# Features of one batch by seven products, a thirtieth seven-product block, tap 0 in two column parts, and engine orders as a table

## The chip, the cores and the metric

The kernel runs on one core of a Trainium2 chip. A core has five engines that run side by side and meet only at semaphores: TensorE (PE; its weight loads are PEld in the profile), VectorE (DVE), ScalarE (ACT), GpSimd (POOL) and SyncE (SP), which here only issues DMAs. The metric is the device time of one execution in microseconds. Before the change it is 252.21 us, the median of 3 runs from 251.29 to 252.40 us.

## The reference

```python
B, T, D, K, U = 2, 4000, 512, 5, 8
h = sum(xp[:, i:i+T, :] @ w1[i] for i in range(5))        # 5 taps over 4000 rows
h = gelu(h)[:, ::2, :]                                    # 2000 rows stay
f = sum(hp[:, i:i+T1, :] @ w2[i] for i in range(5))
f = gelu(f)[:, ::2, :]                                    # 1000 rows stay
fe = f @ w_f                                              # (2, 1000, 512)
ge = g @ w_g                                              # (2, 8, 512)
j = tanh(fe[:, :, None, :] + ge[:, None, :, :])           # (2, 1000, 8, 512)
out = j @ w_o                                             # 16,000 rows of 512
```

All tensors are bf16. Two convolutions with stride 2 make the features `f`; a joint net adds eight vectors `ge` to each feature row, takes tanh and multiplies by `w_o`. The 16,000 joint rows are 125 tiles of 128.

## The kernel before

Activations stand transposed, channels on the 128 partitions and time along the columns, so that every product is a chain of matmuls over four channel blocks `k`, once for each output block `m`. The helper `mm` (L442) records such a chain as one op.

- **First rows of batch 0, directly.** Rows of `x` come in two pieces, `xr0` (128 partitions, 512 KB) and `xr1` (90 partitions, 360 KB). PE turns them with 32 small transposes (L520) into PSUM banks 4 to 7; two DVE copies (`xr0`) and two ACT copies (`xr1`) bring them to `xs`. Then the five taps run in the order 0, 4, 2, 1, 3, each as 16 matmuls of 432 columns (216 even and 216 odd outputs), summed in banks 0 to 3 (`direct`, L702).
- **The other rows.** `Triple` and `Unit` compute three neighbouring outputs of a stride-2, 5-tap convolution from nine chains instead of fifteen, with sums of inputs (`row`) and sums of weights (`w_x`, `w_t`) that DVE and ACT make first. Four triples do the first convolution, two the second; each has four units, one for each `m`. A unit writes PSUM, DVE adds (L530, L429), ACT applies gelu (L434).
- **Features.** `fe` multiplies `fT` by `w_f`: 4 output blocks times 2 time halves, each 4 matmuls of 501 columns, and one copy to `feT` by DVE (L755) or ACT. For batch 0 this stage stands between the convolutions and the joint stage; for batch 1 its eight chains, like the last three units of batch 1 ("conv pieces"), are put between joint blocks.
- **Joint.** ACT makes `tanh(feT + geT)` (L434, `jT` and `jX`), 64 stretches of 1000 columns. `Plain` multiplies one tile of 128 rows by `w_o`: 4 matmuls of 512 columns, one eviction. `Seven` does four tiles by a 2 by 2 block scheme with 7 products instead of 8: 28 matmuls of 256 columns. It needs four sums of tanh blocks (`ss`, L931, DVE or POOL), four sums of `w_o` blocks (`tw`, made once), three products that are copied to `sn` first (L862, L863), three DVE additions `og <- acc, sn` (L429) and one cast. There are 29 `Seven` blocks and 9 plain tiles, three of these at the end.

**Order of the work.** Every op is recorded in program order with its engine (or, in `flex`, a choice of engines), reads, writes and a cost. `edges` (L124) finds what has to wait for what. `schedule` (L175) is a list scheduler: it always takes the engine that can go on first and the most urgent op that is ready there; PE takes the earliest in program order. A string of nudges, one character an op, shifts the urgency. `emit` writes each engine's list with semaphore waits. An engine works through its list strictly in order.

Ops recorded with `pl.port = True` (the sums `ss` here) are planned so that DVE's and POOL's don't overlap (L226 to L231).

Of the kernel before, what the change touches and what calls it, by code (L numbers as in the profile page):

```python
# [50 lines left out]
class Psum:  # L51
# [6 lines left out]
    def pair(self, lo, step, n):  # L58
        ap = self.h[:, lo:lo + 2 * step].rearrange("p (s c) -> p s c", s=2)[:, :, 0:n]
        cells = np.unique(np.concatenate([np.arange(lo, lo + n), np.arange(lo + step, lo + step + n)]) // 512)  # L60
        return View(ap, cells, True)


class Op:
# [4 lines left out]
NUDGES = (  # L69
    "WWWWWWWWWWWWWWWWWWWWWWWWWWWWWWWWWWWWWWWWWWWWWWWWWWWWWWWWWWWWWWWWWWWWWWWWWWWWWWWZGRxV4s1q-S-zIwUDlPB1btjPJVWAWWfYOS-0KT0d"  # L70
    "dIkA-0yl2ZWWWWWWWWWWWyWWQEqWWMWWm8ddCa1B0-yn00WoWW2KtWW7WWPWWg8HCWeWW1mZWWDWW0WWakaF--VX-W0WWOrTWWXWWUWW5WwWWJ-4WW_WW-WW"
    "-5T00vmWGWW70RWW6WW-WWb-mtW4WWGlgWW0WW0WW6-a2YwvXTWiWWKSvWWsWWaWW0W-WW-n-WWcWW_WWjsHUAloWWWWWW5Jd-Pq-WBWWD-2WW4WWeWWw-S0"
    "0fmDvt3RUh-W-WWY--WW-WWAWWEX4iYejb0992kFIky15WNWW2tUWW6WWkWWfuUox0NRL-GW-WW_S8WWSWW4WW0-z4Oe-ByzWdWWh-eWWrWWXWWnLu0W0WWi"
    "8-WWHWWKWWBJ0VxX26uWSWWf1RWW-WWPWWTW-WWtS4WW1WWjWW9WWWW-Zk-d0WYWWq-pWWOWWWWWcO-AWNWW0pSWWQWWzWWPqIYZ---bW4WWi06WW-WW-WWl"
    "WWWWyWW46MD-WW7_0WlW0MW-W-eWZWwnW0Wb0WW_WWXWhWfWWrW-i0-S2VEu4WWsWWbWW0WW9qj9BWWqWW-WWWMe0z0WWoWWKWWWWW4WWsy092WWSWWWWWWL"
    "WWWWWZWW-WW-WWnWWSW0O-SrWWaWWZWWWHWWW8rzw6WWxWW-WWDWWkWWOwFlY6-WWPWWIWWWhWWWWWuoeb4WWYWWYWWiWWqWW7H3IDWWGWWIWWWsWW-n2WWy"
    "WWRWW0WW_WW9W4tRWWCWWLWWWEWWWWW00-X-WWpWWUWWxWWQWWjcm7aWW0WWqWWW-WWWGqTWWoWW-WWlWW-WFQ7DiWWEWWVWWW-WWWW00-g_sjWWUWW0WW-W"
    "W-WyN---WW-WW3WWWTWWc0zz-WWHWWwWWGWWsWp9TM-WWzWWLWWW0WWWyfWWDWW2WWAWWQWE7E0kWW-WWjWWW0WduWW0WWAWW4WWUWpxUpFWWlWW3WWWdWWW"
    "WWwWWOWWJWWLWlzPsiWWzWWoWWWyWg0EOWWqWWAWWqWW9E9XdWWNWW0WWWIWWWNG0-yKWWsWW8WWEWWbI0LPWW-WW6WWW0W1yWW8WWTWWhWWsI_qTWWqWWQW"
    "WWPWWWwBWW-WWrWW-WWpYyqiWWDWWZWWWUW49WW7WWdWWFWWp5_FFWWQWWWWWW6WWWdXE0WWLWWAWWrWW07LstWWWWWtWWWsWxEBY8cWW3WW1WWwWWOVPnsW"  # L80
    "W0WWJWWWOWWWGEWW0WWYWW-WWHCX_fWWmWWCWWW0WC4WWVWWFWWJWW0W-WW-j0WWrWWaWWWWW5WZ-WWfWWFWW1WWOWqW--rmWW5WWdWWWJWWWG-lSWWTWWPW"
    "WbWW0Rrw1WW-WWqWWWDWeXsFWW0WWpWWfWW82Id5WWkWWPWWW8WWW6EWWiWWYWWMWW7W1tSWWdWWkWWWeWx2WW3WW-WWMWWSUx45WWyWWYWWWFWWWWW3WWyW"
    "W-WWfWxWD-qzWW0WWJWWWcWWWTWWtWWrWWyWNWWWWzWWJWWW1WWUWW3WWXWWWhWW0WLWWiW")


class Plan:
# [88 lines left out]
    def schedule(self, pred):  # L175


        ops, HOP = self.ops, self.HOP
        n = len(ops)
        succ = [[] for _ in ops]  # L180
        for i, p in enumerate(pred):
            for j in p:
                succ[j].append(i)
        span = [o.cost + (4.0 if o.dma else 0.0) for o in ops]
        late, nextpe = [0.0] * n, 0.0
        for i in range(n - 1, -1, -1):
            t = min([late[s] - (HOP if pred[s][i] else ops[i].cost - span[i]) for s in succ[i]], default=0.0)
            if ops[i].eng == "pe":
                t = min(t, nextpe)
            late[i] = t - span[i]  # L190
            if ops[i].eng == "pe":
                nextpe = late[i]
        nudge = [0.1 * (ALPHABET.index(c) - 32) for c in NUDGES] if len(NUDGES) == n else [0.0] * n
        left = [len(p) for p in pred]
        ready = [0.0] * n
        free = {e: 0.75 for e in ("pe", "act", "dve", "pool", "sp")}
        cand = {e: [] for e in free}

        def engines(i):
            return ops[i].alt or (ops[i].eng,)  # L200

        for i in range(n):
            if not left[i]:
                for e in engines(i):
                    cand[e].append(i)
        order = {e: [] for e in free}
        wire, lock, start = 0.0, 0.0, [0.0] * n
        for _ in range(n):
            best = None
            for e, c in cand.items():  # L210
                if c:
                    t = max(free[e], min(ready[i] for i in c))
                    if best is None or t < best[0]:
                        best = (t, e)
            t, e = best
            now = [i for i in cand[e] if ready[i] <= t + 0.02]
            i = min(now, key=(lambda i: i) if e == "pe" else (lambda i: (0.15 * i + nudge[i], i)) if e in ("sp", "pool") else (lambda i: (late[i] + nudge[i], i)))
            for f in engines(i):
                cand[f].remove(i)
            order[e].append(i)  # L220
            o = ops[i]
            if o.alt:
                o.eng, (o.fn, o.cost), o.alt = e, o.alt[e], None
            start[i] = t
            free[e] = t + o.cost
            if o.port:  # L226
                if lock > t - 0.2 and e == "dve":
                    free[e] = max(t, lock) + o.cost + 0.2
                elif lock > t:
                    free[e] = lock + o.cost  # L230
                lock = free[e]  # L231
            end = free[e]
            if o.dma:
                wire = max(wire, t + 1.8) + o.wire
                end = max(wire, t + 2.0)
            for s in succ[i]:
                ready[s] = max(ready[s], end + HOP if pred[s][i] else free[e])
                left[s] -= 1
                if not left[s]:
                    for f in engines(s):  # L240
                        cand[f].append(s)
        self.start = start
        self.end = max(free.values())
        return order

    def emit(self, block, tail):
        nc, ops = self.nc, self.ops
        pred = self.edges()
        order = self.schedule(pred)
# [71 lines left out]
def bass_standalone__seq2seq_rnn_t_joint__speech_kernel(  # L321
# [25 lines left out]
    NA, N3 = 216, 262  # L347
# [9 lines left out]
    with ExitStack() as es:  # L357
# [33 lines left out]
        xq = [Buf(nc, f"xq{i}", [6, NK, 288], BF16, v.end - v.bytes) for i, v in enumerate((xs[1], w2_sb))]  # L391
# [22 lines left out]
        tw = at("tw", [4, 2, NT // 2], FP16, wg_sb.end - wg_sb.bytes)  # L414
        assert tw.end <= wg_sb.end
# [61 lines left out]
        came = [load_xr(rt) for rt in range(2)]  # L477
        act(warm[0:1], warm[1:2], ACT.Gelu_apprx_tanh)

        def load_w1(i):  # L480
            src = w1[i].rearrange("(k c) d -> c k d", c=P)
            if len(came) == 2:
                h = D // 2
                for sl in (slice(0, h), slice(h, D)):
                    o = pl.dma("sp", lambda e, sl=sl: e.dma_start(w1_sb[i, :, sl].ap, src[:, :, sl]), (), (w1_sb[i, :, sl],), nbytes=262144)
            else:
                o = load_w("sp", w1_sb[i], src)
                o.after.append(came[-3].idx)
# [657 lines left out]
```

## Time and profile before

| | |
|---|---|
| median of 3 runs | 252.21 us (251.29 to 252.40) |
| profiled execution | 252.07 us |
| its span on the core | 250.3 us |
| PE / DVE / ACT / POOL busy | 245.5 / 207.8 / 209.9 / 106.7 us |
| first tap matmul starts | 7.29 us |
| batch 0's features on PE | 119.0 to 125.8 us |
| POOL sums `ss` / DVE sums `ss` | 86 / 30 instructions |

The span is the time from the first to the last instruction; 1.8 us of the execution lie around it. Busy time counts an instruction from its start to its modelled end; instructions that overlap on an engine are counted once. So 32 chained matmuls that are started every 0.21 us show as one busy stretch, and the rate is read from the starts.

### The profile page before, as it was taken

How to read it: one execution, taken by the hardware profiler on the slowest of the kernel's cores; microseconds unless marked ns; L12 is line 12 of the kernel's file. 1: busy time of each engine (PE TensorE's matmuls, PEld its weight loads, DVE VectorE, ACT ScalarE, POOL GpSimd, SP SyncE). 2: the span in 40 equal slices, each digit the busy share in tenths (PEclk: the TensorE clock that was granted, in tenths of full speed). 3: DMA queues.
4: the chain of work that ended last, by engine and by line, in shares of the span. 5: the costliest groups of instructions: out<-in, count | busy, mean ns of one | idle time of the engine just before them, and what ended most of it. 6: DMA issues, size and time to landing. Idle time of an engine off the chain costs nothing.

```text
span 250.3 us, 5204 instructions
## 1 busy us (share of the span) xinstructions
PE 245.5 (98%) x1920; PEld 184.5 (74%) x1920; DVE 207.8 (83%) x346; ACT 209.9 (84%) x354; POOL 106.7 (43%) x109
## 2 busy tenths in 40 slices
PE   8999999999999999999999999999999999999995
PEld 4556888887666666667467878877778888888873
DVE  1599999968999997981528978899899999999763
ACT  2297799978969868963699998999999999999673
POOL 1000000000000000002429898598998999998910
PEclk9999999999999999999999999999999999999999
DMA  7999999988500052000002223422344444564547
GB/s 212 307 187 173 192 164 212 147 173 262 163 0 3 0 169 85 1 1 3 0 0 84 86 84 105 151 88 84 112 145 131 160 154 141 171 211 156 185 162 240
DMA packets 57392, 31.92 MB, mean 128 GB/s; under 512 B 33837, under 2 KB 57149, under 8 KB 57367
## 3 DMA queue, kind: packets, MB, share of 16 engines
q1 hardware_dynamic: 57367, 31.59, 48.2%
q8 instruction: 15, 0.25, 0.4%
q14 instruction: 10, 0.08, 0.1%
HBM read 7.71 MB, written 16.38 MB: 96 GB/s over the span
## 4 chain that ended last, share of the span: by engine, by line
PE 89%; DVE 4%; DMA 4%; ACT 1%; issue 1%; DVEq 0%
PE acc L442 89%; DMA w_sb<-in_w_dram 2%; DMA xr<-in_x_dram 1%; DVE ssum L429 1%; DVE ssum L530 1%; DVE w_t L429 1%; DVE row L429 1%; ACT hT L434 1%; ACT w_x L434 0%; ACT ost L434 0%; DVE w_x L429 0%; ACT sd L434 0%; DVEq L282 0%
## 5 line engine op out<-in xcount | busy, mean ns | idle before, releaser
L429 DVE TENSOR_TENSOR og<-acc,sn 128x512 bf16<-128x512 f32 x87 | 56.7, 680 | 5.4 <-PE acc L442 4.7
L434 ACT ACTIVATE jT<-feT,geT 128x1000 bf16<-128x1000 f32 (+6 forms) x56 | 51.3, 961 | 0.5 <-DVE feT L755 0.4
L442 PE MATMUL acc<-tw,ss 128*128 128x256 f16 x348 | 48.3, 273 | 0.0
L442 PEld LDWEIGHTS acc<-tw,ss 128*128 128x128 f16 x348 | 33.7, 98 | 7.0 <-issue 0.4
L931 POOL TENSOR_TENSOR ss<-jT 128x512 f16<-128x512 bf16 x26 | 31.4, 1218 | 11.8 <-ACT jT L434 9.2
L442 PE MATMUL acc<-row,w_sb 128*128 128x334 bf16 (+1 forms) x192 | 33.1, 295 | 0.0
L862 ACT ACTIVATE sn<-acc 128x512 f32<-128x512 f32 x51 | 30.6, 619 | 2.6 <-PE acc L442 2.3
L442 PE MATMUL acc<-wo_sb,jT 128*128 128x256 bf16 (+1 forms) x196 | 31.6, 288 | 0.0
L426 POOL MEMSET hT<- 128x8 bf16 (+2 forms) x6 | 0.7, 149 | 71.6 <-ACT hT L434 66.7
L442 PE MATMUL acc<-row,w_x 128*128 128x262 bf16 (+1 forms) x192 | 28.5, 290 | 0.2 <-ACT sd L434 0.2
L434 ACT ACTIVATE jX<-feT,geT 128x1000 bf16<-128x1000 f32 (+4 forms) x28 | 25.0, 919 | 0.0
L442 PEld LDWEIGHTS acc<-row,w_sb 128*128 128x128 bf16 x192 | 18.5, 98 | 6.7 <-DVE acc L530 0.3
L442 PEld LDWEIGHTS acc<-row,w_x 128*128 128x128 bf16 x192 | 18.6, 98 | 6.1 <-ACT sd L434 0.5
L442 PEld LDWEIGHTS acc<-wo_sb,jT 128*128 128x128 bf16 x196 | 19.1, 98 | 5.3
L434 ACT ACTIVATE sd<-acc 128x334 f32<-128x334 f32 (+1 forms) x48 | 20.3, 429 | 2.6 <-PE acc L442 2.1
L530 DVE SCALAR_TENSOR_TENSOR acc<-acc,sd 128x334 f32<-128x334 f32 (+1 forms) x24 | 11.6, 482 | 11.4 <-PE acc L442 11.4
L434 ACT ACTIVATE hT<-acc 128x262 bf16<-128x262 f32 (+2 forms) x36 | 15.4, 433 | 6.7 <-PE acc L442 6.6
L863 DVE COPY sn<-acc 128x512 f32<-128x512 f32 x26 | 17.6, 682 | 3.9 <-PE acc L442 3.9
L931 POOL TENSOR_TENSOR ss<-jX 128x512 f16<-128x512 bf16 x17 | 20.3, 1209 | 1.2 <-ACT jX L434 0.7
L931 POOL TENSOR_TENSOR ss<-jT,ss 128x512 f16<-128x512 bf16 x15 | 17.8, 1191 | 1.0 <-DVE ss L931 0.7
L442 PE MATMUL acc<-wo_sb,ss 128*128 128x256 bf16 x116 | 17.7, 273 | 0.0
L931 POOL TENSOR_TENSOR ss<-ss,jT 128x512 f16<-128x512 f16 x15 | 17.5, 1173 | 0.6 <-DVE ss L931 0.4
(105 smaller groups left out, 499.7 us busy)
## 6 DMA issues: line engine op xcount, KB each, us to landing
out_dram<-og SPq DMA_DIRECT2D x44, 256.0 KB, 2.2
w_sb<-in_w_dram SPq DMA_DIRECT2D x9, 512.0 KB, 5.1
out_dram<-og SPq DMA_DIRECT2D x14, 128.0 KB, 2.2
out_dram<-ost SPq DMA_DIRECT2D x7, 128.0 KB, 2.0
xr<-in_x_dram SPq DMA_DIRECT2D x1, 512.0 KB, 3.4
w_sb<-in_w_dram SPq DMA_DIRECT2D x2, 256.0 KB, 5.3
wf_sb<-in_w_f_dram SPq DMA_DIRECT2D x1, 512.0 KB, 3.7
wg_sb<-in_w_g_dram SPq DMA_DIRECT2D x1, 512.0 KB, 4.7
```

The lines of the kernel that those rows point to most:

```text
L426: pl.op("pool", lambda e: e.memset(v.ap, 0.0), (), (v,))
L429: pl.op(eng, lambda e: e.tensor_tensor(out=o.ap, in0=a.ap, in1=b.ap, op=op), (a, b), (o,), 0.02 + 2.14e-3 * o.ap.free_size() if eng == "po ...
L434: pl.op("act", lambda e: e.activation(o.ap, i.ap, func, scale=scale, bias=0.0 if bias is None else bias.ap), rd, (o,), o.ap.free_size() * ...
L442: ins = e.matmul(o.ap, lhsT=l.ap, rhs=r.ap, start=start and n == 0, stop=stop and n == len(pairs) - 1, skip_group_check=not check)
L530: pl.op(eng, lambda e: e.scalar_tensor_tensor(out=o.ap, in0=a.ap, scalar=f, in1=b.ap, op0=ALU.mult, op1=add), (a, b), (o,), vec_cost(o, (a ...
L862: pl.flex({"act": (lambda e: e.activation(o.ap, v.ap, ACT.Copy), 0.05 + n * 0.833e-3), "dve": (lambda e: e.tensor_copy(out=o.ap, in_=v.ap) ...
L863: "dve": (lambda e: e.tensor_copy(out=o.ap, in_=v.ap), 0.065 + n * 1.04e-3)}, (v,), (o,))
L931: fn = lambda e, o=S[i], x=x, y=y, op=op: e.tensor_tensor(out=o.ap, in0=x.ap, in1=y.ap, op=op)
```

## The change

1. **Tap 0 and the first loads.** The loads are issued as `xr0`, the first two channel blocks of tap 0's weights, `xr1`, the other two blocks, and then tap 4 without a wait; before, they were `xr0`, `xr1`, two column halves of tap 0, and tap 4 after `xr0` had landed. Tap 0 is done in columns 0 to 127 and 128 to 215 of each output half, and each in two halves of the channel blocks: 16 matmuls of 256 and 16 of 176 columns. The transposes of `xr1` stand inside it. The copies of even rows (`turn(0, 0)`, `turn(1, 0)`) are DVE's, those of odd rows ACT's.
2. **Features of batch 0** by a new class `Feature`, the 2 by 2 scheme with seven products: for each of two `m`, seven products of 2 matmuls with 504 columns. It needs four sums of feature blocks (DVE, 1008 elements), four sums of `w_f` blocks (`wfsums`, 512 elements, DVE or POOL), six PSUM results kept in `sn`, six DVE additions and two plain copies.
3. **Thirty `Seven` blocks** and 5 plain tiles instead of 29 and 9.
4. **Orders as a table.** `schedule` and the nudges go; `ORDER` lists each engine's ops by their numbers, two characters each.
5. `ge` is recorded two slots earlier, and the sums of `w_o` may be DVE's too.

Read with the ops' numbers in program order, the table begins as follows. PE: 8 warm-up matmuls, transposes of even and odd rows of `xr0`, tap 0 columns 0 to 127 (blocks 0, 1), transposes of `xr1`, tap 0 columns 0 to 127 (blocks 2, 3), tap 0 columns 128 to 215, taps 4, 2, 1, the `t2` chains of units 0 and 2, tap 3 with the `t2` chain of unit 1 in it, then the units, strongly mixed. ACT: the warm-up, `w_x[1]` of block 0, `w_t[1]` of blocks 0 and 1, the copy of `xr0`'s odd rows, `w_x[1]` of block 1, the copy of `xr1`'s odd rows. DVE: the two copies of even rows, then 15 weight sums, then the first row sum of triple 0. In the joint stage DVE has 50 of the sums `ss` and POOL 70; of the 90 copies to `sn` ACT has 56 and DVE 34; of the 30 casts to `og` ACT has 20 and DVE 10. Of the eight weight sums of `w_f` and `w_o`, POOL has two.

In the feature stage PE's order is: unit 5.0's `t1` and `s1`, then p1, p2, p5, p6 for m = 0, p1 for m = 1, p3 for 0, p2, p5, p6 for 1, p7 for 0, p3, p7 for 1, unit 5.1's `t2`, p4 for 0, unit 5.0's `t0`, p4 for 1, unit 5.0's `ti`, the first half of block S0's p1, `si`, the second half, `s0`, and then the first plain tile. DVE's is: feature sum 1, unit 5.0's first addition, feature sums 2 and 3, unit 5.0's second, the results k0 first half, k0 second half, k1 first half, one copy to `sn`, k2, k1, k3 second halves, k2, k3 first halves. ACT's is: five copies to `sn` with one gelu among them, and tanh of (v0, k0), (v1, k0), (v0, k1), (v0, k2), (v0, k3).

```diff
-NUDGES = (
...
+ORDER = {
+    "pe": (
+        "0X0Y0Z0a0b0c0d0e0f0h0l0m0n0o0p0r0t0u0v0w0x0y0z0_0-101112131415161718191A1B1C1D1E1s2o1F1G2O1H1I1u1v2y2V2W2Q2R352q2r2z"
...
-    def schedule(self, pred):
...
+    def schedule(self):
+
+        order = {k: [64 * ALPHABET.index(a) + ALPHABET.index(b) for a, b in zip(s[::2], s[1::2])] for k, s in ORDER.items()}
...
+        FQ = NT3 // 2 + 1
+        ft = at("ft", [4, 2, 3, FQ], BF16, ss[1].end - ss[1].bytes)
+        fs = at("fs", [4, 2, NT // 2], FP16, ss[3].end - ss[3].bytes)
...
-        came = [load_xr(rt) for rt in range(2)]
+        came = [load_xr(0)]
+        load_w1(0, 2, (0,))
+        came.append(load_xr(1))
+        load_w1(0, 2, (2,))
         act(warm[0:1], warm[1:2], ACT.Gelu_apprx_tanh)
...
+        load_w1(4)
+        for i in (2, 1, 3):
+            load_w1(i)
...
+        turn(0, 0, "dve")
+        turn(0, 1, "act")
...
+        for q0, n in ((0, P), (P, NA - P)):
+            for ks in ((0, 1), (2, 3)):
+                for m in range(NK):
+                    mm(ps.pair(m * NT + q0, NA, n), [(w1_sb[0, k, m * P:(m + 1) * P], both(0, k, q0, n)) for k in ks],
+                       q0 == 0 and ks[0] == 0, False, False)
+                if q0 == 0 and ks[0] == 0:
+                    turn(1, 0, "dve")
+                    turn(1, 1, "act")
+        for i in taps[1:]:
+            for m in range(NK):
+                direct(i, m)
...
+        class Feature:
...
+            def sums(self, late):
+                f = self.B
+                for i, x, y in (((1, f[1, 1], ft[0]), (2, f[1, 1], f[0, 1]), (3, f[1, 0], ft[1])) if late else ((0, f[0, 1], f[0, 0]),)):
+                    shared(ft[i], x, y, sub, False)
...
+                mm(ps.cols(bk * NT, 3 * FQ), [(lhs(k), rhs(k)) for k in range(2)], start, True, False)
...
+                if s is None:
+                    evict(None, o, cut(v))
+                else:
+                    tt("dve", o, cut(v), cut(s), add)
...
-        first = [lambda h=h, m=m: fe(0, h, m) for m in range(NK) for h in range(2)]
+        f0 = Feature(0)
+        f0.sums(False)
+        f0.p1(0)
+        f0.p5(0)
         piece()
...
+        for m in range(2):
+            f0.p2(m)
+            f0.p3(m)
+            f0.p6(m)
+            f0.c12(m)
+            tanhs(0, 0, 1)
+        for m in range(2):
+            f0.p7(m)
+        for m in range(2):
+            f0.p4(m)
+            tanhs(0, 0, 1)
         piece(3)
...
-        gaps = (6, 12)
-        NEND = ntile - (2 + 4 * S1 + 4 * 14 + 2 * len(gaps))
+        gaps = ()
+        NEND = ntile - (2 + 4 * S1 + 4 * 15 + 2 * len(gaps))
...
-        for n in range(14):
+        for n in range(15):
```

## The prediction

> **What bounds the kernel now.** I read the page first, its busy times and the chain that ended last.
>
> ```profile
> PE 245.5 (98%) x1920; PEld 184.5 (74%) x1920; DVE 207.8 (83%) x346; ACT 209.9 (84%) x354; POOL 106.7 (43%) x109
> ...
> PE 89%; DVE 4%; DMA 4%; ACT 1%; issue 1%; DVEq 0%
> ```
>
> TensorE is busy 98% of the span and owns 89% of the chain. Since a busy PE may still be starved, I next read the chain in order of time, for where PE is not the cause.
>
> ```profile
> 4.20 5.55 DMA w_sb<-in_w_dram
> ...
> 21.38 0.63 ACT w_x L434
> 22.01 1.26 ACT hT L434 x3
> 23.27 0.29 ACT sd L434
> 23.56 0.05 issue
> 23.61 223.79 PE acc L442 x1788
> ```
>
> Up to 23.6 us the end is set by tap 4's weights (landed at 9.75), then by DVE's and ACT's weight sums. From there to 247.4 it is one unbroken stretch of matmuls. Then the timeline of the start, and that of batch 0's features.
>
> ```profile
> 4.58 2.17 PE L520 MATMUL acc<-ident,xr 128*128 128x128 bf16 x32
> ...
> 5.67 1.29 DVE L527 COPY xs<-acc 128x1024 bf16<-128x1024 bf16 x2 [4.54 <-PE acc L520]
> 6.46 1.44 ACT L434 ACTIVATE xs<-acc 128x720 bf16<-128x720 bf16 x2 [4.23 <-PE acc L520]
> ...
> 7.29 1.09 PE L442 MATMUL acc<-xs,w_sb 128*128 128x432 bf16 x5 [0.54 <-ACT xs L434]
> ```
>
> Tap 0 waits 0.54 us for ACT's copy of the second piece of rows.
>
> ```profile
> 119.02 6.63 PEld L442 LDWEIGHTS acc<-fT,wf_sb 128*128 128x128 bf16 x32
> ...
> 121.78 1.13 ACT L434 ACTIVATE jT<-feT,geT 128x1000 bf16<-128x1000 f32 x1 [0.39 <-DVE feT L755]
> ...
> 125.77 0.59 PEld L442 LDWEIGHTS acc<-row,w_sb 128*128 128x128 bf16 x4
> ...
> 135.33 0.86 PEld L442 LDWEIGHTS acc<-tw,ss 128*128 128x128 f16 x8
> ...
> 136.21 0.43 PEld L442 LDWEIGHTS acc<-wo_sb,jT 128*128 128x128 bf16 x4
> ```
>
> Two rates come from the starts of weight loads: 32 matmuls of 501 columns in 125.77 - 119.02 = 6.75 us, 0.211 us each or 0.421 ns a column; 8 of 256 columns in 136.21 - 135.33 = 0.88 us, 0.110 us each. PE runs at these rates, so its time falls only if columns go, or if one of its few waits goes. Last, the engine table of the features and of the joint stage:
>
> ```profile
> 118.00:126.00 8.00, 8.00 (x43) 3.89 (x41) 3.72 (x7) 5.50 (x9) 3.66 (x4) 1.00 0.00 0
> 126.00:246.00 120.00, 120.00 (x1002) 97.16 (x1001) 104.93 (x172) 113.74 (x181) 100.23 (x86) 1.00 0.40 131
> ```
>
> Columns are PE, weight loads, DVE, ACT, POOL. In the joint stage DVE is busy 87%, ACT 95%, POOL 84%: little is spare there.
>
> **The change part by part.** The profiled execution took 252.07 us (span 250.3, 1.8 around it), 0.14 below the median of 252.21; the sum is made against 252.07.
>
> *Features.* Removed: 32 matmuls of 501 columns, 6.75 us. Added: 28 of 504, at 0.421 ns a column 28 x 0.212 = 5.94 us. PE: -0.81. DVE and ACT get 14 evictions instead of 8, and DVE four sums of 1008 elements. Nearest row for the sums: row sums of 1048 elements, 0.70 us alone and 0.60 from start to start in a row. The eight weight sums depend on loads alone; DVE does six (0.41 us each, 2.5 us) about 105 to 120, where it is busy 8.0 of 15 us: hidden, and 2.5 us on the path if that gap fills.
>
> On the path is DVE's list. Call the first feature product's start T. Unit 4.3's last product ends at T - 1.1 (unit 5.0's two chains lie between), its gelu at T - 0.5. Then DVE does a sum, a unit addition, two sums, a second addition (0.60, 0.41, 0.60, 0.60, 0.41, the first addition not before T + 0.2): T + 2.2. Results at 0.59 each: k0 complete at T + 3.4, k1 at T + 5.8, k3 at T + 7.9. ACT's tanh takes 1.05 us of 1000 columns (4.19 us for four from 126.72): (v0, k0) from T + 3.5, against T + 2.76 before; (v0, k3) ends at about T + 9.2. PE reaches the plain tile that needs it after 14 products (5.94), four unit chains of 0.57 before S0's p1 and between its halves, the halves (0.44) and one more 0.57: T + 9.2. So the cover is just used up; a wait of 0.1 us, and 1.0 us if DVE's results cost 0.70 each (the row of its feature copies: two in 1.41 us) instead of 0.59. I take 0.1, since DVE works back to back here, and keep 0 to 1.0. Behind that waiting tile stands all of the joint stage on PE.
>
> *Thirtieth block.* Removed: four plain tiles, 16 x 512 columns x 0.421 ns = 3.45 us. Added: 28 x 0.110 = 3.08 us. PE: -0.37. The evictions rise by 3 (seven for four) and the sums `ss` by 4; SP issues two stores of 256 KB for four of 128 KB, and DMA is 40% busy: nothing.
>
> *Tap 0.* The first DVE copy ends near 5.67 + 0.65 = 6.3 and frees the first part; 7.29 before. But the columns are the same, and the transposes of the second piece (0.65 us) now lie behind the start: 6.4 + 0.88 + 0.65 + 0.88 + 16 x 176 x 0.421 ns (1.19) = 10.0, against 7.29 + 16 x 0.183 = 10.2. The loads allow it: the first piece landed 3.4 us after its issue at 0.74, and the four first transfers keep their bytes, the last landing near 7.5 before. Tap 4's weights, landed at 9.75, are now issued some 1.5 us sooner; 8.2 to 9.75 is in time for 10.0. PE: -0.2, bounds -0.4 and 0.
>
> *Orders up to 25 us.* ACT's second op is now a weight scaling that waits for DVE's fifth weight sum; queued behind it are the copies of odd rows that tap 1 needs at 10.0 + 32 x 0.183 = 15.9. Sums of 0.60 from about 9.3 and the landing of tap 2's weights put that scaling at 12.1 to 12.4; then 0.6, 0.96, 0.9, 0.53 and 0.65 us of ACT: 15.9 to 16.3. A wait of 0 to 0.4. On the other side lie the waits at 23.2 and 24.9 us, where weight loads idle 0.45 and 0.24 us, some 0.45 us of product time lost; the `t2` chains drawn ahead of tap 3 give these sums more time, though DVE is full from 10 to 50 us as before. I take -0.3 together, bounds -0.5 and +0.4.
>
> *Other orders.* From 25 us on PE lost nothing but its rate; a new order can win at most a few tenths and can lose wherever a list stands still. I take 0; the loss is the third case below. The tail (last matmul at 247.4 to the end at 250.3) stays.
>
> Sum: -0.81 - 0.37 - 0.2 - 0.3 + 0.1 = -1.6 us: 250.5 on the profiled execution's scale, 250.6 on the median's.
>
> **A rule against it.** DVE's sums `ss` are the row to look at.
>
> ```profile
> L931 DVE TENSOR_TENSOR ss<-jT x11: 412/426/907, 125.9 to 232.8; 128x512 f16<-128x512 bf16 x11
> L931 DVE TENSOR_TENSOR ss<-ss,jT x4: 424/1313/1357, 129.4 to 164.2; 128x512 f16<-128x512 f16 x4
> L931 DVE TENSOR_TENSOR ss<-jT,ss x4: 415/914/1086, 143.4 to 237.6; 128x512 f16<-128x512 bf16 x4
> ```
>
> The same sum takes 0.41 or up to 1.36 us; all 30 take 20.8 us, 0.69 on average. POOL's take 1.2. The Trainium skill ("SBUF — State Buffer", section "SBUF: two separate sides") says why: a DVE instruction with two SBUF inputs and a GpSimd one exclude each other for a whole instruction. By that rule alone, with POOL busy 70% and half a POOL sum to wait, the 50 sums would average 0.83 us, an estimate that would put the time far above the forecast; the trace agrees on the blocking, but 0.69 at a POOL share of 84% says that planned starts avoid half of it.
>
> **The rivals.**
>
> *Late cover, no change.* DVE's results at 0.70 (+0.9), tap 1's wait of 0.4 and no gain around 23 us (+0.7 in all) leave 250.6 + 1.6 = 252.2. For it: both chains meet PE's need to 0.1 us. Against: each uses the slower of two rows.
>
> *DVE becomes the bound of the joint stage, slower.* Its other work there is 104.9 - 20.8 = 84.1 us; three more additions, three casts, two copies less add 4 x 0.60 = 2.4. With 50 sums of length s it needs 86.5 + 50 s. It has 119.6 us, of which the fullest stretch before (185 to 230 us) used 97%: 115.6. It decides from s = 0.58. At 0.41 DVE is not the bound; at 0.69 the need is 121.0 and the stage grows by 121.0/0.967 - 119.6 = 5.5 us: 256. With POOL at 70 sums instead of 86 the excess of 0.28 over 0.41 shrinks to 0.23, s = 0.64, and the stage grows by 2.9: 253.5. Against it: an isolated DVE eviction counts 0.68 and one in a row 0.60, so that a full DVE gets back some 5 us, which moves the deciding point to about 0.68. ACT's load is the same, five copies more and six casts less.
>
> **How the numbers follow.** Forecast 0.57: columns surely go, and no row has the covers gone. Late cover 0.17; DVE as the bound 0.26, since s = 0.64 lies just under where it decides. 0.5% of the median is 1.26 us, about what a measurement can tell from no change: faster is under 250.95, slower over 253.47; faster 0.57, same 0.17, slower 0.26. The forecast's own range is 249.7 (all waits gone) to 251.0. The range of all takes in the late cover and about a third of the third case: 249.6 to 254.5.
>
> **What would show it.** First tap matmul at 6.4 and tap 0 done at 10.0; feature products of 504 columns in 5.9 us; first long tanh 3.5 us after them; PE without holes from 25 us to its end near 245.8. Wrong if PE starts thin out after 135 us with DVE sums near 0.7 us or DVE over 97% (third case), or if the plain tile or tap 1 waits over half a microsecond (second).

## The result, and the profile after

The changed kernel takes 253.03 us (median of 9 runs, 251.94 to 255.57) beside 252.04 us for the kernel before (median of 9, 251.29 to 252.40): a ratio of 1.0061, 95% interval 1.0033 to 1.0088. It is slower by 0.6% (0.4% by the medians), with an interval that leaves out no change, where the prediction was 250.6 us and faster. The profiled execution took 253.25 us, with a span of 251.5 us (250.3 before). Here and below, medians and ranges are over all executions, and ratios leave out the few that took over 1.5% longer than the fastest of the same kernel.

The page of the changed kernel, busy times and the chain by engine:

```profile
PE 245.4 (98%) x1942; PEld 185.6 (74%) x1944; DVE 222.7 (89%) x385; ACT 209.3 (83%) x354; POOL 85.5 (34%) x91
...
PE 78%; DVE 9%; DMA 5%; ACT 3%; issue 2%; SPq 1%; DVEq 0%
```

PE is as busy as before (245.5), but its share of the chain fell from 89% to 78%: VectorE, the loads and ScalarE now set the end in places where nothing but PE did. Three places carry it. The first is the start. The chain in order of time:

```profile
1.65 0.52 SPq L438
2.21 0.39 SPq L452
2.64 6.62 DMA w_sb<-in_w_dram
9.28 6.48 DMA w_sb<-in_w_dram
15.78 0.69 DVE w_x L399
...
19.48 0.62 DVE row L399
20.15 4.88 PE acc L412 x32
```

The chain runs through tap 4's weights (landed at 9.26) and then tap 3's, which are issued at 9.28 and land at 15.76; before, tap 3's landed at 14.52. PE's weight loads, with their idle time in brackets:

```profile
16.50 2.68 PEld L412 LDWEIGHTS acc<-xs,w_sb 128*128 128x128 bf16 x16 [0.84 <-ACT xs L404]
20.15 0.78 PEld L412 LDWEIGHTS acc<-row,w_x 128*128 128x128 bf16 x8 [0.96 <-DVE row L399]
```

The waits of SP's queue in the first 16 us (us in total, times, longest):

```profile
SPq L452 <- DMA xr<-in_x_dram: 4.2, 1, 4.2
```

Tap 1 waits 0.84 us for the copy of `xr1`'s odd rows, the first `t2` chain 0.96 us for VectorE's first row sum. SP stands 4.2 us until `xr1` has landed (7.27 us, 5.67 before), and only then issues tap 2's weights: in this program the sixth, seventh and eighth load (taps 2, 1 and 3) each wait for an earlier one to land (`xr1`, the second half of tap 0's weights, tap 4's weights).

The second place is the features of batch 0 and the conv unit ahead of them:

```profile
116.99 0.40 PEld L412 LDWEIGHTS acc<-row,w_sb 128*128 128x128 bf16 x4 [0.54 <-DVE acc L504]
...
121.78 0.13 PEld L412 LDWEIGHTS acc<-ft,fs 128*128 128x128 f16 x2 [0.38 <-DVE acc L504]
...
125.64 0.11 PEld L412 LDWEIGHTS acc<-ft,fs 128*128 128x128 f16 x2 [0.75 <-DVE sn L838]
...
130.31 0.55 PEld L412 LDWEIGHTS acc<-wo_sb,jT 128*128 128x128 bf16 x4 [0.30 <-ACT jT L404]
```

The engine table by stage (PE, weight loads, DVE, ACT, POOL) answers to the two lines shown of before:

```profile
118.00:126.00 8.00, 7.73 (x43) 3.66 (x41) 8.00 (x16) 6.13 (x13) 0.00 (x0) 1.00 0.00 0
126.00:247.00 121.00, 120.51 (x1016) 97.85 (x1016) 112.19 (x201) 115.01 (x181) 80.59 (x70) 1.00 0.39 129
```

VectorE is busy for all of the 8 us around the features, where it was busy 3.72 us, and PE has its first gaps there. The third place is late in the joint stage (223 to 232 us), where four weight loads idle 0.51, 0.24, 0.27 and 0.16 us.

An idle weight load is not all lost, since products still run under it. What PE loses is read from the starts of its products: the time from one start to the next, less what its columns take. One trap lies in this reading: a product that the trace did not record looks like a loss. At the first plain tile there are four weight loads (the line at 130.31 above) but three products:

```profile
130.54 0.81 PE L412 MATMUL acc<-wo_sb,jT 128*128 128x512 bf16 x3 [0.18 <-issue]
```

The product before began at 130.06 and the first recorded one of the tile at 130.54, 0.34 us more than the columns of the product before take; 0.22 of that is the product that is missing from the trace, and the loss is 0.12. (In g3 below, whose trace has all four, the loss at this place is 0.12 by starts.) For the changed kernel the losses are then 0.58, 0.70 and 0.32 in small pieces up to 30 us; 0.36, 0.09, 0.43 and 0.12 from 116 to 131 us; 0.42, 0.13, 0.15 and 0.08 from 224 to 232: 3.4 us. Before it was 0.84 (0.34 and 0.13 near 24 us, three of 0.09 to 0.15 later). With the predicted -1.18 of columns and -0.22 at the start (first tap matmul at 6.42 instead of 7.29, with 0.65 us of transposes now behind it) the sum is +2.54 - 1.40 = +1.1 us, against +1.2 between the spans. The gain came; waits took it and more.

### The profile page after: what moved, and what is told of

It is laid out like the page before. It is cut to its first block, busy times and chain, and to the rows that moved or that the text cites. A ratio compares the mean times of both kernels' runs of the same rounds, so it can differ in the third digit from the quotient of the medians.

```text
span 251.5 us, 5268 instructions
## 1 busy us (share of the span) xinstructions
PE 245.4 (98%) x1942; PEld 185.6 (74%) x1944; DVE 222.7 (89%) x385; ACT 209.3 (83%) x354; POOL 85.5 (34%) x91
## 4 chain that ended last, share of the span: by engine, by line
PE 78%; DVE 9%; DMA 5%; ACT 3%; issue 2%; SPq 1%; DVEq 0%
PE acc L412 78%; DMA w_sb<-in_w_dram 5%; DVE row L399 2%; ACT hT L404 2%; DVE hT L399 1%; DVE acc L504 1%; DVE ss L906 1%; ACT sn L837 1%; DVE feT L399 1%; DVE w_t L399 1%; DVE ssum L399 1%; DVE og L399 0%; DVE ssum L504 0%; ACT w_sb L404 0%; ACT sd L404 0%
## 5 line engine op out<-in xcount | busy, mean ns | idle before, releaser
L399 DVE TENSOR_TENSOR og<-acc,sn 128x512 bf16<-128x512 f32 x90 | 58.6, 683 | 4.0 <-PE acc L412 3.2
L412 PE MATMUL acc<-tw,ss 128*128 128x256 f16 x360 | 56.3, 273 | 0.0
L837 ACT ACTIVATE sn<-acc 128x512 f32<-128x512 f32 (+1 forms) x61 | 35.0, 605 | 2.8 <-PE acc L412 2.6
L906 POOL TENSOR_TENSOR ss<-jT 128x512 f16<-128x512 bf16 x18 | 20.8, 1165 | 12.8 <-ACT jT L404 9.7
L906 POOL TENSOR_TENSOR ss<-ss,jT 128x512 f16<-128x512 f16 x12 | 14.1, 1175 | 25.0 <-DVE ss L906 22.2
L412 PE MATMUL acc<-wo_sb,ss 128*128 128x256 bf16 x120 | 21.7, 272 | 0.3 <-DVE ss L906 0.3
L906 POOL TENSOR_TENSOR ss<-jX 128x512 f16<-128x512 bf16 x16 | 18.6, 1175 | 5.8 <-PE acc L412 4.3
L838 DVE COPY sn<-acc 128x512 f32<-128x512 f32 (+1 forms) x25 | 16.9, 683 | 3.1 <-PE acc L412 3.1
L412 PE MATMUL acc<-hT,w_sb 128*128 128x334 bf16 x96 | 16.9, 305 | 0.0
L906 POOL TENSOR_TENSOR ss<-jT,ss 128x512 f16<-128x512 bf16 x13 | 15.2, 1173 | 4.9 <-DVE ss L906 4.7
```

Source lines behind the costliest of these rows:

```text
L399: pl.op(eng, lambda e: e.tensor_tensor(out=o.ap, in0=a.ap, in1=b.ap, op=op), (a, b), (o,), 0.02 + 2.14e-3 * o.ap.free_size() if eng == "po ...
L412: ins = e.matmul(o.ap, lhsT=l.ap, rhs=r.ap, start=start and n == 0, stop=stop and n == len(pairs) - 1, skip_group_check=not check)
L837: pl.flex({"act": (lambda e: e.activation(o.ap, v.ap, ACT.Copy), 0.05 + n * 0.833e-3), "dve": (lambda e: e.tensor_copy(out=o.ap, in_=v.ap) ...
L838: "dve": (lambda e: e.tensor_copy(out=o.ap, in_=v.ap), 0.065 + n * 1.04e-3)}, (v,), (o,))
L906: fn = lambda e, o=S[i], x=x, y=y, op=op: e.tensor_tensor(out=o.ap, in0=x.ap, in1=y.ap, op=op)
```

## The experiments

Times are medians. Each kernel is compared with the kernel before on the same chip: 251.9 us beside e1 to e4, 251.75 beside e5 to e8, 251.78 beside f1 to f3 and e9, 252.1 beside g1 to g4, 251.65 beside g5 and g6.

### One part at a time, and the orders

The three parts alone, in the kernel before with its list scheduler; ops that all of them share keep their nudges.

```diff
 f1  + class Feature, wfsums; batch 0's features by seven products
 f2  - gaps = (6, 12) ... range(14)
     + gaps = () ... range(15)
 f3  + load_xr(0), load_w1(0, 2, (0,)), load_xr(1), load_w1(0, 2, (2,)), load_w1(4); tap 0 in two column parts
 e8  (changed kernel)  - ORDER = {...}   + def schedule(self, pred) of before, no nudges
 e9  (kernel before)   + nudge = [0.0] * n
```

> Kernel before, with its list scheduler, and only batch 0's features by seven products (nudges kept for the ops that stay). Theory F (this stage is bound by DVE and ACT, not by PE: six copies more, four sums and the w_f sums put 0.9 us or more of waiting behind the 0.8 us of products saved): 252.2 to 253.5, with a wait of 0.8 to 1.5 us ahead of the first plain tile or among the products. Theory G (the part pays by its columns, the table spoils it): 251.0 to 251.4.

> Kernel before, with its list scheduler, and only the thirtieth block in place of four plain tiles (nudges kept where ops match). By columns 251.5 to 251.7. If the joint stage lacks ACT and DVE time (three evictions and four sums more): 252.0 to 253.0, with PE waits after 220 us.

> Kernel before, with its list scheduler, and only tap 0 in parts with the new order of loads. If the load order is what loses (second piece of rows lands at 7.2 to 7.8 us instead of 5.3 to 5.7, tap 3's weights 1.2 us later): tap 0 starts at 6.4, but DVE's row sum comes late and PE waits 0.5 to 1.5 us between 20 and 26 us: 252.2 to 253.2. If the written-out order is needed for that wait, the list scheduler goes round it: 251.5 to 251.8.

> Kernel before with all nudges at zero: what the list scheduler gives without tuned urgencies, as a measure for the run of the changed program under it (256.4). If order alone is worth little: 252 to 253, and the parts are what cost the other 3 to 4 us; if order is worth much: 254 to 256.

> The changed program (features by seven products, thirty blocks, tap 0 in parts, its loads), but with the list scheduler of the kernel before, without nudges, instead of the table. If the table's order is what loses: 251.0 to 252.5, since a list scheduler never leaves an engine idle in front of an op that is ready. If the parts themselves lose, the features' chain above all: 253 to 255, with a wait of over 1 us at the end of the features.

| | us (range) | ratio, 95% interval |
|---|---|---|
| f1, features alone | 254.93 (254.79 to 264.35) | 1.0125, 1.0109 to 1.0142 |
| f2, thirtieth block alone | 256.77 (256.51 to 257.20) | 1.0202, 1.0185 to 1.0220 |
| f3, tap 0 and loads alone | 252.55 (251.98 to 253.32) | 1.0030, 1.0015 to 1.0045 |
| e9, before without nudges | 253.00 (252.59 to 253.40) | 1.0045, 1.0031 to 1.0060 |
| e8, all parts, list scheduler | 256.38 (255.77 to 256.65) | 1.0177, 1.0159 to 1.0195 |

No part alone gains anything. Features alone, PE's weight loads:

```profile
124.96 0.11 PEld L446 LDWEIGHTS acc<-ft,fs 128*128 128x128 f16 x2 [1.95 <-ACT sn L867]
...
131.19 0.76 PEld L446 LDWEIGHTS acc<-wo_sb,jT 128*128 128x128 bf16 x5 [1.22 <-ACT jT L438]
```

Start to start, PE loses 1.63 and 1.11 us at these two places (the second without a product of 0.22 us that the trace lacks), 2.7 in all, and the kernel is 3.1 us slower: in this order the seven-product stage of 6 us doesn't feed itself. In f3 the losses are 0.65 and 0.58 us near 23 us, where the kernel before lost 0.47. f2 is not a price of the block: its PE ends 2 us later than before, but its span is 5 us longer, and SP's longest wait at the end says why:

```profile
SPq L979 <- DVE ost L867: 3.0, 1, 3.0
```

The cast that this line names ended at 248.99, after the store was issued (248.69); what the store waited for is VectorE's addition before it, which ended at 248.66. SP issues nothing for 2.7 us until then, and after it nine more stores one after the other, 0.4 to 0.5 us each, until 253.4; in the kernel before it had two left after PE's end, until 248.2. That is the order of one list, so f2 leaves open what the thirtieth block costs. e9 says that nudges are worth 1.2 us to the kernel before, and e8 that the table is worth 3.4 us (256.38 against 253.03) to the changed one beside a scheduler without nudges. f1 to f3 carry nudges that were tuned for another program, so that each prices a part and an untuned order together; the changed program with a scheduler tuned for it was not run.

### The first 20 us

Two edits of the table (an entry names an engine, an op and where it goes: ahead of which op on which engine). e1 takes the two copies of odd rows ahead of ScalarE's first weight scaling, e3 loads `xr1` before the first half of tap 0's weights.

```diff
+MOVES = (('act', 44, 'act', 97), ('act', 54, 'act', 97))        # e1
+MOVES = (('sp', 8, 'sp', 7),)                                   # e3
```

> Changed kernel, but in ACT's list the two copies of odd rows stand ahead of the first weight scaling, so that they no longer wait for DVE's fifth weight sum. Theory A (the lists meet PE's need to a tenth of a microsecond; late loads and blocked DVE instructions therefore reach PE as many small waits, and those are where the gain went): the 0.84 us wait of tap 1 vanishes, but PE then reaches the first t2 chain earlier, whose row sum DVE delivers no sooner, so that wait grows from 0.96 to about 1.5 us: 252.6 to 253.1. If waits simply added: 252.4. Theory B (ACT and DVE are the bound of the joint stage, and whatever PE gains earlier comes back there as waits): 253.0.

> Changed kernel, but the second piece of rows is loaded ahead of tap 0's first weights, as before the change. Theory A: that piece lands near 5.7 instead of 7.27 us, tap 2's weights, which are issued after it, go out 1.5 us sooner, and tap 3's weights land near 14.6 instead of 15.76; DVE's wait of 0.62 us for them goes and the first row sum comes 0.6 to 1.2 us sooner; PE's 0.96 us wait at 20.15 falls to 0 to 0.4 and tap 1's 0.84 a little; the start of tap 0 stays within 0.3 us: 252.0 to 252.6. Theory B: 253.0.

e1: 253.83 us (253.61 to 254.00), ratio 1.0071 (1.0054 to 1.0088), not better. Tap 1's wait of 0.84 is gone and the `t2` chain's grew from 0.96 to 1.80: tap 1's wait was covered by the later one. e3: **251.59 us** (251.33 to 254.82; nine of ten runs at most 251.91), ratio **1.0000** (0.9974 to 1.0027). SP's waits for `xr1` and then PE's weight loads in e3:

```profile
SPq L457 <- DMA xr<-in_x_dram: 2.1, 1, 2.1
```

```profile
15.01 3.58 PEld L417 LDWEIGHTS acc<-xs,w_sb 128*128 128x128 bf16 x20
18.67 0.95 PEld L417 LDWEIGHTS acc<-row,w_x 128*128 128x128 bf16 x8
```

`xr1` lands at 5.22 instead of 7.27, tap 2's weights at 9.89 instead of 11.37, tap 3's at 13.12 instead of 15.76, and both waits are gone. One swap in SP's list, with the same bytes, is worth 1.4 us: the load order alone makes the difference between slower and the same.

The link from `xr1` to tap 3's weights is looser than that to tap 2's. The `t2` wait ends 4.4 us after tap 3's weights have landed: 15.76 and 20.15 in the changed kernel, 16.50 and 20.89 in e1, 15.90 and 20.30 in e2. But those weights are issued when tap 4's have landed, not `xr1`; in the changed kernel they went out sooner than before (9.28, 9.77) and took 6.48 us instead of 4.75, with the loads of taps 2 and 1 issued 2.0 and 1.4 us ahead of them instead of 4.1 and 2.2. That the crowding makes them late is likely and not shown: with the rows first they land at 13.1 to 14.7 us in eight of the profiled executions, and at 15.1 to 16.7 in three (e5, e7, g1).

### The unit ahead of the features

In the changed kernel GpSimd does two of the eight weight sums at 111 us. VectorE's timeline there, and GpSimd's:

```profile
111.42 3.54 DVE L399 TENSOR_TENSOR hT<-hT 128x1336 bf16<-128x1336 bf16 x2
```

```profile
111.13 1.39 POOL L994 TENSOR_TENSOR tw<-wo_sb 128x512 f16<-128x512 bf16 x1 [8.46 <-DVE sd L399]
112.48 1.77 POOL L994 TENSOR_TENSOR fs<-wf_sb 128x512 f16<-128x512 bf16 x1
```

Two row sums, 0.84 us each when alone, take 3.54 us beside GpSimd's two; the unit addition after them is late, and with it PE's product at 116.99. e2 gives both sums to VectorE, e4 is e1, e2 and e3 together, g1 is e2 and e3.

```diff
+MOVES = (('pool', 620, 'dve', 621), ('pool', 626, 'dve', 695))  # e2
```

> Changed kernel, but the two weight sums that POOL makes at 111 to 114 us (one of w_f, one of w_o) are DVE's, the first just ahead of the next w_f sum, the second after the features. Theory A: POOL's two sums block DVE's two row sums of batch 1 (3.54 us for two instead of 1.6), and this makes DVE late for unit 4.3 and the features; without them the two row sums take 1.6 to 1.7 us, PE's waits at 117.0 and 118.2 us (0.54 and 0.20) vanish and those among the feature products (0.38, 0.24, 0.32, 0.75) halve: 251.8 to 252.5. Theory B: no gain, 253.0, since the joint stage waits instead.

> Changed kernel with all three edits: copies of odd rows first, both weight sums on DVE, second piece of rows first. Theory A: the waits up to 21 us (1.8 us of idle weight loads) and most of those from 117 to 126 us (2.4 us) go together: 250.6 to 251.6, under the kernel before, and no new wait in the joint stage. Theory B: 252.5 to 253.0, and PE's waits after 130 us grow by what was won before.

> Rows first (251.59) with GpSimd's two weight sums given to VectorE as well. Theory (each product time that PE loses before the joint stage reaches the end one to one): the start-to-start loss of 0.36 us at U4.3's t0 goes, the feature stage's losses (0.09, 0.44, 0.34) stay, 251.2. Rival (the joint stage takes it back): 251.6 if the feature stage waits longer by as much, about 253 to 254 if the joint stage falls into the waits of 1.07, 0.45, 0.33 and 0.65 us at 214 to 222 that the same edit had without the rows first.

e2: 253.53 us (252.68 to 256.03), ratio 1.0079 (1.0040 to 1.0118). The waits at 117 us are gone, but new ones of 1.07, 0.45, 0.33 and 0.65 us stand at 214 to 222 us. e4: 252.90 (251.30 to 254.30), 1.0033 (1.0007 to 1.0060). Its profiled execution (251.53) has neither the waits at the start nor those at 117, and is no faster than e3's 251.59: the wait at p7 of m = 1 lost 0.60 us instead of 0.44, and tap 0 started later. g1: 252.84 (251.16 to 256.25), 1.0017 (0.9986 to 1.0048): four of its ten runs lie at 251.16 to 251.38, as the theory has it, and four at 252.7 to 253.2, where the rival has them. Both happen, so the edit settles nothing for the median.

### The waits that come and go at 214 us

In e2's trace the addition that opens these waits (213.25) writes an `og` block that two stores read last, issued at 208.55 and 209.10. They landed 4.6 and 4.7 us later, the first at 213.13, just ahead of the addition that reuses its half; the same stores take 2.6 and 3.0 us in e3 and 2.6 and 3.3 in the changed kernel, without those waits. There are three `og` blocks. e5 is e3 with a fourth, e6 is e3 with the feature stage in another order (all products but p4 together right ahead of p4, so that unit 5's chains come first; the four sums of `w_o` after the features; GpSimd's two sums on VectorE; ScalarE's copies ahead of its tanh), e7 is e6 with the fourth block.

```diff
-og = [at(f"og{i}", ...) for i in range(3)]
+og = [at(f"og{i}", ...) for i in range(3)] + [at("og3", [4, NT], BF16, jT.end)]    # e5, e7
+MOVES = (('sp', 8, 'sp', 7), ('pe', 629, 'pe', 663), ... ('dve', 624, 'dve', 695), ... ('act', 687, 'act', 676))    # e6, e7
```

> Second piece of rows first (as in the run that reached 251.6), and a fourth output block in the ring that joint blocks write and stores read. Theory C (a store that lands late, 4.7 us after its issue instead of 2.2, holds the DVE addition that writes its block again, three blocks later, and through it PE; this is what spreads the runs): the median stays at 251.3 to 251.6, and no run lies over 252.5. Theory D (the waits in the joint stage come from DVE and POOL sums that exclude each other, not from stores): times and spread as without the fourth block.

> Second piece of rows first, and the feature stage's lists loosened: PE's products in the order p1, p5 of m = 0, p1 of 1, p2 of 0, p5 of 1, p6, p3 of 0, p2, p6, p3 of 1, p7 of 0, the t2 chain, p7 of 1; the copies to sn all on ACT; DVE's results ahead of its third feature sum and of unit 5.0's addition; the sums of w_o behind the features, the w_f sum of POOL on DVE. Theory A (waits by lists without slack): the waits at 115.4 and 116.5 us (0.54, 0.20) and among the products (0.38, 0.24, 0.32, 0.76) go, the plain tile comes 1.2 to 2.0 us sooner: 249.8 to 250.6. Theory B (the joint stage is bound by ACT and DVE): the plain tile comes sooner, but PE waits in the joint stage and the time is 251.3 to 251.8.

> The loosened feature stage and the fourth output block together, second piece of rows first. Theories A and C: 249.8 to 250.5 and no run over 251.5. Theory B: 251.3 to 251.8.

| | us (range) | ratio, 95% interval |
|---|---|---|
| e5, rows first, four blocks | 251.74 (251.57 to 254.28) | 1.0021, 0.9995 to 1.0047 |
| e6, rows first, looser features | 254.42 (254.16 to 256.05) | 1.0116, 1.0083 to 1.0150 |
| e7, both | 252.93 (252.41 to 254.32) | 1.0053, 1.0035 to 1.0072 |

e6 has the late store (4.6 us) and the waits at 214 to 222 (1.03, 0.45, 0.34, 0.65), and e7 has neither: with the fourth block the median is 1.5 us lower than without it, and no lower in e5 than in e3. How the block does it stays open, since in e7's profiled execution the two stores landed after 2.6 and 3.1 us: no trace shows a fourth block taking up a late one. It does not remove the spread of the runs: e5's profiled execution took 253.36 us and has the waits of the first 25 us back (0.53 at tap 1, 0.98 at `t2`) with the rows loaded first, since tap 3's weights landed at 15.88. So this table turns a late landing into time at two places. And a looser order did not help the features:

```profile
125.35 0.11 PEld L417 LDWEIGHTS acc<-ft,wf_sb 128*128 128x128 bf16 x2 [1.19 <-DVE feT L404]
...
130.63 0.40 PEld L417 LDWEIGHTS acc<-row,w_t 128*128 128x128 bf16 x4 [1.18 <-ACT sd L409]
```

In e6 the waits of 0.38, 0.24, 0.32 and 0.75 us became one of 1.19 for VectorE and one of 1.18 for ScalarE. The waits were only moved: from 125 to 131 us VectorE and ScalarE are each busy for 5.1 of 6 us.

### Taking the work away

To price the two late places at the end, work is left out of e3. g2: the six additions of feature results do 24 columns of some 500 (GpSimd clears the rest of `feT` early on). g3: GpSimd's sums `ss` from the 21st block on do 16 columns of 512 (the expectation says 32; the trace has 16). g4: both.

```diff
-tt("dve", o, cut(v), cut(s), add)
+few = lambda w: w.map(lambda a: a[:, 0:8])
+pl.op("dve", lambda e: e.tensor_tensor(out=few(o).ap, in0=few(cut(v)).ap, in1=few(cut(s)).ap, op=add), ...)    # g2, g4
+early = pl.ops[546]                                    # g2, g4: GpSimd's clearing of the tail of hT
+early.fn = lambda e: (e.memset(feT[0][0:NK].ap, 0.0), fn0(e))[1]
+if self.n >= 20: brief = lambda e, ...: e.tensor_tensor(out=o[:, :, 0:8], ...)    # g3, g4
-alt = {"pool": (fn, 1.12), "dve": (fn, 0.34)}
+alt = {"pool": (brief, 1.12), "dve": (fn, 0.34)}
```

> Rows first (251.59), and VectorE's six additions of the feature results work on 24 of their columns, so that the output is not the reference's: this takes some 3.5 us of VectorE out of the feature stage and leaves every wait in place. Theory (VectorE bounds the stage): the losses at p7 of m = 1 (0.44) and at the plain tile (0.34) go, those at 115 and 120 us and in the joint stage stay: 250.8. Rival (ScalarE bounds it, with five copies and five long tanh before the plain tile): the plain tile still waits 0.3 and the time is 251.2 to 251.6. Second rival (what is won is given back in the joint stage): no wait in the stage, and still 251.4 or more.

> Rows first (251.59), and GpSimd's sums for the blocks from the 21st on work on 32 of 512 columns, so that the output is not the reference's; VectorE's sums are whole. Theory (VectorE's sum behind a GpSimd sum, 1.29 us instead of 0.41 for the 24th block at 222.3, makes PE wait at 223 to 230): the losses there (0.42, 0.13, 0.15, 0.08) go, about 250.9. Rival (ScalarE's copies to sn, which the profile names at that wait): no change, 251.4 to 251.7.

> Both shortenings, output not the reference's in the same two places. Theory (the forecast was right on the columns, and what it missed are these waits): 250.0 to 250.3, under the forecast of 250.6. Rival (another limit stands close behind): 250.8 or more.

| | us (range) | ratio, 95% interval |
|---|---|---|
| g2 | 255.04 (253.23 to 258.40) | 1.0100, 1.0016 to 1.0185 |
| g3 | 251.62 (250.88 to 252.72) | 0.9989, 0.9966 to 1.0011 |
| g4 | 253.14 (252.72 to 257.31) | 1.0062, 1.0023 to 1.0101 |

g2 and g4 came out slower for a reason that the edit brought in. GpSimd's timeline in g2, and VectorE's:

```profile
100.77 3.44 POOL L1216 MEMSET feT<- 128x4008 f32 x1 [36.27 <-ACT hT L409]
```

```profile
104.34 0.85 DVE L404 TENSOR_TENSOR row<-hT 128x1336 bf16<-128x1336 bf16 x1 [2.58 <-POOL hT L401]
```

The clearing stood ahead of a small one of `hT` for which VectorE waits, and PE lost 1.96 us start to start at 107.2. g3 did what its theory said: of the four late waits only 0.16 is left, and four of its runs lie at 250.88 to 251.02. In e3 VectorE's sum there, GpSimd's beside it, and then VectorE's same sum in g3:

```profile
222.26 1.29 DVE L911 TENSOR_TENSOR ss<-jX,ss 128x512 f16<-128x512 bf16 x1
```

```profile
222.12 3.55 POOL L911 TENSOR_TENSOR ss<-jX 128x512 f16<-128x512 bf16 x3
```

```profile
223.54 0.42 DVE L911 TENSOR_TENSOR ss<-jX,ss 128x512 f16<-128x512 bf16 x1
```

So the wait that the profile puts down to "ACT sn" (that copy had ended at 222.93, PE began at 223.66) was for this sum, which ended at 223.55. But g3's own profiled execution has another one of 1.14 us at 213.6, behind the first of the two late stores (4.6 us):

```profile
DVE og L404 <- DMA out_dram<-og: 1.2, 1, 1.2
```

g5 and g6 are g2 and g4 with the clearing behind the small one.

```diff
-early.fn = lambda e: (e.memset(feT[0][0:NK].ap, 0.0), fn0(e))[1]
+early.fn = lambda e: (fn0(e), e.memset(feT[0][0:NK].ap, 0.0))[0]
```

> As g2_feature_results_short (VectorE's six additions of the feature results on 24 of their columns, output not the reference's), with the clearing of feT behind the clearing of hT on GpSimd and not ahead of it, so that VectorE's row sums no longer wait for it. The start-to-start loss of 1.96 us at U4.1's t0 goes. In g2 the stretch from the first feature wait to the last product was 0.45 us shorter than with the rows first alone (122.24 to 248.19 against 120.14 to 246.54). Theory (that passes to the end): 251.59 - 0.45 = 251.1. Rival (the stage's remaining waits grow when PE comes sooner): 251.5 or more.

> As g4_both_short (also GpSimd's sums from the 21st block on at 32 of 512 columns, output not the reference's in both places), with the same clearing moved. From the plain tile's start to the last product g4 took 117.11 us against 117.86 with the rows first alone: 0.75 less. Theory (the two add up): 251.59 - 0.45 - 0.75 = 250.4, near the forecast of 250.6. Rival: 250.9 or more.

g5: 251.37 us (251.06 to 253.68), ratio 1.0002 (0.9983 to 1.0021); seven of twelve runs lie at 251.06 to 251.41, around the 251.1 of the theory, five at 252.1 to 253.7. By the intervals neither g3 nor g5 differs from the kernel before, so that each place has its price from the traces alone. g6: **250.74 us** (250.33 to 251.28), ratio **0.9960** (0.9946 to 0.9975), faster than the kernel before by 0.9 us where the theory had 250.4. Feature waits and the stage table of g6:

```profile
124.00 0.11 PEld L417 LDWEIGHTS acc<-ft,fs 128*128 128x128 f16 x2 [0.41 <-DVE sn L843]
...
128.57 0.55 PEld L417 LDWEIGHTS acc<-wo_sb,jT 128*128 128x128 bf16 x4 [0.19 <-ACT jT L409]
```

```profile
118.00:126.00 8.00, 8.00 (x44) 3.85 (x42) 5.75 (x16) 6.27 (x11) 0.00 (x0) 1.00 0.00 0
```

With VectorE at 5.75 of 8 us PE has no gap left in the table's view; start to start it loses 0.09 us at p7 of m = 1 (0.44 in e3) and 0.01 at the plain tile (0.12 in e3; both without the product that the traces lack, which the expectations above still count in their 0.34). What is taken out of both places does reach the end, and with the rows first it brings the time to the forecast's 250.6. These kernels leave work out, so they are prices and no version to use; no complete kernel here beat the one before.

## Why the prediction was wrong

The forecast was 250.6 us, by columns saved and covers that hold. The columns were saved, and the covers failed: 2.5 us of new losses where the prediction put -0.2 (+0.1 and -0.3). Of the late-cover rival (252.2) two terms came, and larger than priced, the wait at tap 1 and no gain near 23 us; its wait of 1.0 us at the plain tile did not.

- **Features, PE.** Right: 14 products of 504 columns at 0.212 us a matmul, 0.81 us saved.
- **Features, "eight weight sums ... hidden".** Failed. The prediction named 2.5 us on the path if their gap fills, and it did fill: VectorE is busy 15.97 of the 16 us from 104 to 120. Two of them stand on VectorE's path just ahead of the feature sums (first feature product T = 120.31):

```profile
119.72 0.42 DVE L994 TENSOR_TENSOR tw<-wo_sb,tw 128x512 f16<-128x512 bf16 x1
120.05 0.41 DVE L994 TENSOR_TENSOR fs<-wf_sb,fs 128x512 f16<-128x512 bf16 x1
120.39 0.67 DVE L994 TENSOR_TENSOR ft<-fT,ft 128x1008 bf16<-128x1008 bf16 x1
```

  The sum that could begin with unit 4.3's gelu (ended at 119.96) begins at 120.39. From there the list ran with results at 0.63 us each, not 0.59 (the rival's 0.70): k0 complete at T + 4.0 (predicted 3.4), k1 at T + 6.5 (5.8), k3 at T + 8.6 (7.9), first long tanh at T + 4.3 (3.5), and the one that the plain tile needs done at T + 9.95 (9.2). Every link is 0.6 to 0.8 us late. And GpSimd's two, costed at nothing, blocked the row sums of unit 4.3 (3.54 us for two): 0.36 us of PE.
- **Features, "a wait of 0.1 us".** Right for the plain tile, by luck, and failed for the stage. The plain tile lost 0.12, but the tanh that it needs came 0.75 us late and PE came 0.7 late too (T + 9.9, predicted 9.2), for it had waited elsewhere: 0.43 us at p7 of m = 1. That loss was on no path of the prediction: p7 adds into the bank of p6, whose copy to `sn` is VectorE's and stands behind three results in its list; with the results short (g6) it is 0.09. The prediction followed one consumer, the plain tile, and none of the products. Together with the 0.36 ahead of it and 0.09 at 121.8 the stage loses 1.0 us, more than the 0.81 that it saves.
- **Thirtieth block and the sums `ss`.** -0.37 of columns came. "The sums `ss` rise by 4 ... nothing" was not borne out: 0.78 us was lost at 224 to 232 us, and g3 and g4, where 0.08 of it is left, show VectorE's sum blocked by GpSimd's as the cause. Whether the block's four sums bring that about, or only where the table puts all 120, no run separates.
- **Tap 0.** Right in its own terms: start 6.42, tap 4's first product at 10.08 (tap 0 done at 10.0 predicted), tap 4's weights at 9.26. "**The loads allow it**" failed. It asked when the first four transfers land as a group (7.88, predicted near 7.5), not which of them SP's next issue waits for. `xr1`, now third, lands 1.6 us later; tap 2's weights, which wait for it, come 0.15 us later, and tap 3's 1.24.
- **Orders up to 25 us, -0.3.** Failed in size and sign: 1.60 us lost in place of 0.47, so +1.1, outside the bounds of -0.5 and +0.4. Tap 1's wait was seen (0 to 0.4; it was 0.84 idle and 0.58 lost). That of the `t2` chain for tap 3's weights, by way of VectorE's first row sum, was not. e3, which changes the load order alone, undoes it: 1.4 us.
- **Other orders, 0.** Not borne out, and not priced apart: from 30 us on PE lost 0.37 us before and 1.8 now, which is what the points above count at the features and at 224 to 232 us. That the table is worth 3.4 us over a scheduler without nudges doesn't say what it is worth over a tuned one.
- **VectorE as the bound of the joint stage (0.26).** Not so. It was to decide at a mean of 0.58 us for the sums `ss`; the 50 of them take 24.5 us, 0.489 on average (0.696 before). Two of the groups:

```profile
L906 DVE TENSOR_TENSOR ss<-jT x20: 415/418/1387, 130.4 to 239.1; 128x512 f16<-128x512 bf16 x20
L906 DVE TENSOR_TENSOR ss<-jX,ss x7: 415/418/1289, 181.9 to 237.5; 128x512 f16<-128x512 bf16 x7
```

  The table starts 38 of the 50 while no sum runs on GpSimd (9 of 30 before), but three take over 1.0 us. By g3 and g4 the mechanism cost PE 0.7 us, not 2.9.

The Trainium skill ("SBUF — State Buffer", section "SBUF: two separate sides") has a VectorE instruction with two SBUF inputs and a GpSimd one that reads SBUF exclude each other for the whole of an instruction: the 1.29 us of e3 against 0.42 us of g3 for the same sum, with nothing changed but GpSimd's columns, agree with it.

## What to carry to other kernels

When loads are reordered, follow the issue queue, not only the bytes: ask for every later load which landing releases it, and what that one's landing becomes. When a product is traded for sums and additions on another engine, lay out that engine's whole list in the stage, small precomputed sums included, and check every product that waits for it, not just the last consumer; here the stage in which that engine was busy all the time gave back more than it saved. A fully ordered table can turn a late landing into time, so price it on late landings as well as on the usual ones. And when losses are read from starts, count the products first: one that the trace lacks reads as a wait.

## What the runs showed of the hardware

- A load of 360 KB landed 4.5 us after its issue behind the other rows (issued at 1.19), and 5.6 us when it was issued at 1.65 behind a weight load of 256 KB, which itself took 3.8 us: half a microsecond in the issue became 1.6 us in the landing.
- Two stores of 256 KB at 207 to 209 us, half a microsecond apart, took 2.6 and 3.0 to 3.3 us in the profiled executions of the changed kernel, e3 and g6, and 4.6 and 4.7 us in those of e2, g3 and g5, where the median store takes 2.2. In each of the late ones VectorE's next addition into the first one's block began 0.1 us after that landing.
- Two VectorE row sums beside two GpSimd sums took 3.54 us in place of 1.7.
